# Absolute sums in the seven spatial groups: pieces of 512 elements become pieces of 1024, spread over more places

## The chip, the cores and the metric

The kernel runs on one core of a Trainium2 chip. The metric is device microseconds of one execution. The time before is 690.24 us, the median of 3 runs (690.11 to 691.26).

## What is computed

The reference mixes two branches over one input x of 2048 rows and 1024 columns: a dilated local attention (branch A) and a gated spatial MLP (branch B). The change lies in branch B and in how its last product is prepared.

```python
z = gelu(x @ w_in)                    # 2048 x 3584
z1, z2 = z[:, :1792], layernorm(z[:, 1792:])
g = w_sp @ z2 + b_sp[:, None]         # spatial product, 2048 x 2048 by 2048 x 1792
b = (z1 * g) @ w_out                  # 1792 x 1024
out = s * a + (1 - s) * b             # s = sigmoid(x . gate_w), a = attention
```

## The kernel before

The element product z1 * g is kept in SBUF as bfloat16, in tiles of 128 columns (14 of them, f = 0 to 13). For the first 1024 rows of the output it lies in two buffers, `z1c_slots[0]` and `z1c_slots[1]`, of 14 tiles x 512 rows each; the code calls this half v. For the other 1024 rows it lies in `u_late(f)`, 1024 rows a tile; the code calls this half u.

The last product with w_out uses a scheme of seven block products in place of eight (sums and differences of blocks), in 16-bit floats. To keep these sums in range, each half is first multiplied by a power of two. The power comes from the largest absolute row sum: ScalarE takes the sum of absolute values of each piece of u and v (an ACTIVATE with `ACT.Abs` and `accum_out`; each leaves a second, short instruction that reads the accumulator), VectorE takes the maximum of all pieces, and `whole_power` makes the power of two from it in three steps. The value itself need not be exact: it is a bound, and the scale is undone in `omg`.

Program order is fixed by hand (`tc.manual_schedule`): each engine runs its instructions in the order in which the code issues them, and waits for others by semaphores. Some work is handed out by `beat`, which keeps a planned time and issues an item when that time is reached; the absolute sums of the attention output (L412, 512 elements each) come in this way.

The change lies in the stage of `seven_products(n, extra)`, n = 0 to 6, the "spatial groups". A group computes tiles n and n + 7 of g for the last 1024 rows with seven products (L920) of eight matmuls each, all on TensorE:

1. product 1 into bank `pa`; ScalarE copies `pa` to `pb` (L943)
2. product 2 into `pe`; ScalarE copies it to `e5` (L945); then `extra(n, 1)`
3. product 3 adds to `pb`, so it waits for the copy L943; ScalarE copies `pb` to `pc` (L951), then fills two banks for the next group (L777)
4. product 4 adds to `pa`; ScalarE casts it to `gsb` (L956); then the u sums of the group before (L1012), and VectorE multiplies by z1 (`g_out`, L925); `extra(n, 2)`
5. product 5 adds to `pb`, so it waits until L951 has read it; VectorE adds `e5` (L963); `extra(n, 3)`
6. product 6 adds to `pc`; VectorE adds `e5` (L971); `extra(n, 4)`
7. product 7 adds to `pb`, so it waits until L963 has read it; ScalarE casts it (L980); `extra(n, 5)`

`extra(n, place)` puts other work between these steps: the scaling of w_out (L993) and its block sums on VectorE, loads, and the v sums (L1016). In groups 0 to 4, v sums stand at places 1 and 5, up to three in a row: place 1 for `z1c_slots[0]`, place 5 for `z1c_slots[1]`, tiles 3n to 3n + 2. Group 5 starts with the maximum of the v sums (L1229). The u sums of group n - 1 stand in group n behind L956, four in a row; those of group 6 come after the stage, beside `attn_pair(0)`, whose matmuls are L1127.

All absolute sums also write their absolute values to a scratch that nobody reads: `abs_out` (512 elements) or `abs_wide` (1024). `abs_wide` is used earlier by the row sums of the spatial weights (L848), which are ACTIVATEs of the same function over 1024 elements. Two further ACTIVATE-class lines of 1024 elements are L569 (absolute sums of a weight tile read with a stride) and L291 (a copy that permutes).

Of the kernel before, what the change touches and what calls it, by code (L numbers as in the profile page):

```python
# [10 lines left out]
F32 = mybir.dt.float32  # L11
# [4 lines left out]
P = 128  # L16
# [12 lines left out]
NF = FH // P  # L29
# [28 lines left out]
def kernel(  # L58
# [13 lines left out]
    nc = tc.nc  # L72
# [4 lines left out]
    sm = ctx.enter_context(tc.tile_pool(name="small", bufs=1))  # L77
# [5 lines left out]
    def reg(off, n):  # L83
        return arena[:, off:off + n]
# [13 lines left out]
    def warm_up(widths):  # L98
        pw = psum.tile([P, 512], F32, name="pw", tag="ps")
        for n in widths:  # L100
# [9 lines left out]
    s1 = sm.tile([P, 64], F32, name="s1")  # L110
# [12 lines left out]
    b_in = sm.tile([P, 8], BF, name="b_in")  # L123
    b_up = sm.tile([P, 8], BF, name="b_up")
    w_l1 = sm.tile([P, 7], F32, name="w_l1")
    v_l1 = s1[:, 0:28]
    u_l1 = sm.tile([P, 28], F32, name="u_l1")
    top = sm.tile([P, 1], F32, name="top")
    top_i = sm.tile([P, 1], I32, name="top_i")
    top_b = sm.tile([P, 1], BF, name="top_b")  # L130
# [57 lines left out]
    z1c_slots = [reg(CD_OFF + 8192, 7168).rearrange("p (f t) -> p f t", f=NF),  # L188
                 reg(EF_OFF + 8192, 7168).rearrange("p (f t) -> p f t", f=NF)]
# [3 lines left out]
    abs_out = reg(CD_OFF + 18944, 512)  # L193
    abs_wide = reg(EF_OFF + 15360, 1024)
# [261 lines left out]
    def load_wo(h):  # L456
        sync.dma_start(wo_sb[:, 4 * h:4 * h + 4, :], wo_d[4 * h:4 * h + 4].rearrange("g p n -> p g n"))

    def load_oT(a):
        sync.dma_start_transpose(oT_slots[a % 4], o_d[a * P:(a + 1) * P, :])  # L460
# [319 lines left out]
    def seed_group():  # L780
        seed(bsp_bc[:, 1024:1536])
        seed(bsp_more)
# [57 lines left out]
    def u_late(f):  # L840
        return u_first[:, f // 7] if f % 7 == 0 else z2[:, f - 1, 0:8, :]
# [49 lines left out]
    def t_sums(k):  # L891
        if k == 0:
            TT(t1, b_hi[:, 0:8], b_lo[:, 0:8], ALU.subtract)
        elif k == 1:
            TT(t3, b_hi[:, 8:16], b_hi[:, 0:8], ALU.subtract)
        elif k == 2:
            TT(t2, b_hi[:, 8:16], t1, ALU.subtract)
        else:
            TT(t4, b_lo[:, 8:16], t2, ALU.subtract)
        beat.on_vector(2.3)  # L900

    def s_sum(n, k):
        a11, a12 = z2[:, n, 0:8, :], z2[:, n, 8:16, :]
        a21, a22 = z2[:, n + 7, 0:8, :], z2[:, n + 7, 8:16, :]
        if k == 0:
            TT(sums[0], a21, a22, ALU.add)
        elif k == 1:
            TT(sums[1], sums[0], a11, ALU.subtract)
        elif k == 2:
            TT(sums[2], a11, a21, ALU.subtract)  # L910
        else:
            TT(sums[3], a12, sums[1], ALU.subtract)
        beat.on_vector(0.7)

    def bank():
        return psum.tile([P, 512], F32, name="ps", tag="ps")

    def product(dst, lhs, rhs):
        for k in range(8):
            nc.tensor.matmul(dst[:], lhs[:, k, :], rhs(k), start=False, stop=k == 7, skip_group_check=True)  # L920
        beat.run(8 * 512)

    def g_out(f, c, gsb):
        dst = u_late(f)[:, 4 * (c - 2):4 * (c - 1), :]
        TT(dst, gsb.rearrange("p (a q) -> p a q", a=4), dst, ALU.mult)  # L925
        beat.on_vector(0.43)

    def next_gsb():
        gs[0] += 1
        return gsb_slots[gs[0] % 3]  # L930

    def seven_products(n, extra):
        fa, fb = n, n + 7
        for f in (fa, fb):
            sync.dma_start(u_late(f).rearrange("p (c a) q -> p c (a q)", c=2),
                           z1_d[2:4, :, f * 512:(f + 1) * 512].rearrange("c p t -> p c t"))
        more = n + 1 < 7
        e5 = e5_slots[n % 2]
        extra(n, 0)
        pa, pe = seeded.pop(0), seeded.pop(0)  # L940
        product(pa, z2[:, fa, 0:8, :], lambda k: b_lo[:, k])
        pb = bank()
        nc.scalar.copy(pb[:], pa[:])  # L943
        product(pe, sums[0], lambda k: t1[:, k])
        nc.scalar.copy(e5, pe[:])  # L945
        if more:
            s_sum(n + 1, 0)
        extra(n, 1)
        product(pb, sums[1], lambda k: t2[:, k])
        pc = bank()  # L950
        nc.scalar.copy(pc[:], pb[:])  # L951
        if more:
            seed_group()
        product(pa, z2[:, fa, 8:16, :], lambda k: b_lo[:, 8 + k])
        gsb = next_gsb()
        nc.scalar.copy(gsb, pa[:])  # L956
        if n:
            u_sums(n - 1)
        g_out(fa, 2, gsb)
        extra(n, 2)  # L960
        product(pb, sums[2], lambda k: t3[:, k])
        gsb = next_gsb()
        TT(gsb, pb[:], e5, ALU.add)  # L963
        beat.on_vector(0.7)
        g_out(fb, 3, gsb)
        extra(n, 3)
        product(pc, sums[3], lambda k: b_hi[:, 8 + k])
        if more:
            s_sum(n + 1, 2)
        gsb = next_gsb()  # L970
        TT(gsb, pc[:], e5, ALU.add)  # L971
        beat.on_vector(0.7)
        g_out(fa, 3, gsb)
        extra(n, 4)
        product(pb, z2[:, fb, 8:16, :], lambda k: t4[:, k])
        if more:
            s_sum(n + 1, 1)
            s_sum(n + 1, 3)
        gsb = next_gsb()
        nc.scalar.copy(gsb, pb[:])  # L980
        g_out(fb, 2, gsb)
        extra(n, 5)
# [8 lines left out]
    def w_scale(f):  # L991
        for ff in (f, f + 7):
            nc.vector.tensor_scalar(w_out_sb[:, ff, :], w_out_sb[:, ff, :], w_up[:].bitcast(F32), None, ALU.mult)  # L993
        beat.on_vector(0.9)

    def w_sum(f, k):
        b11, b12, b21, b22 = w_tiles(f)
        if k == 0:
            TT(w_t(f, 0), b12, b11, ALU.subtract)
        elif k == 1:  # L1000
            TT(w_t(f, 1), b22, w_t(f, 0), ALU.subtract)
        elif k == 2:
            TT(w_t(f, 2), b22, b12, ALU.subtract)
        else:
            TT(w_t(f, 3), b21, w_t(f, 1), ALU.subtract)
        beat.on_vector(0.43)

    def u_sums(n):
        for h, f in enumerate((n, n + 7)):
            for k in range(2):  # L1010
                c = 4 * n + 2 * h + k
                nc.scalar.activation(abs_out.rearrange("p (i q) -> p i q", i=4), u_late(f)[:, 4 * k:4 * k + 4, :], ACT.Abs,  # L1012
                                     accum_out=u_l1[:, c:c + 1])

    def v_sum(c, f):
        nc.scalar.activation(abs_out, z1c_slots[c][:, f, :], ACT.Abs, accum_out=v_l1[:, 14 * c + f:14 * c + f + 1])  # L1016

    def u_rows(q, r, half):
        if q < 4:
# [62 lines left out]
    def wo_scale(h):  # L1082
        half = wo_sb[:, :, 512 * h:512 * h + 512]
        nc.vector.tensor_scalar(half, half, wo_up[:].bitcast(F32), None, ALU.mult)
# [127 lines left out]
    def extra(n, place):  # L1212
        if place == 1 and n == 0:
            t_sums(3)
        if place == 0 and n in (1, 3):
            part = slice(0, 11) if n == 1 else slice(11, NF)
            sync.dma_start(w_out_sb[:, part, :], wout_v[:, part, :])
        for k, f in enumerate(scale_sets.get(n, ())):
            if place == 2 + 2 * k:
                w_scale(f)  # L1220
        if place == 0:
            for f in sum_sets.get(n, ()):
                for k in range(4):
                    w_sum(f, k)
        if place in (1, 5) and n < 5:
            for f in range(3 * n, min(14, 3 * n + 3)):
                v_sum(place // 4, f)
        if n == 5 and place == 0:
            nc.vector.tensor_reduce(top[:], v_l1, AX.X, ALU.max)  # L1229
            next(v_steps)  # L1230
        if (n, place) in ((5, 3), (6, 0)):
            next(v_steps)
        if n == 2 and place == 5:
            nc.vector.tensor_reduce(top[:], o_l1[:], AX.X, ALU.max)
            next(o_steps)
        if (n, place) in ((3, 3), (4, 0)):
            next(o_steps)
        if n == 5 and place == 5:
            nc.scalar.copy(z2[:, 13, 0:8, :], u_first[:, 1])
        if n == 6 and place in (1, 2):  # L1240
            load_wo(place - 1)
        if n == 6 and place == 3:
            for r in range(4):
                load_oT(r)
            prepare(0)

    def prepare(q):
        u_scale(q)
        for k in range(4):
            u_sum(q, k)  # L1250
# [31 lines left out]
    for n in range(7):  # L1282
        seven_products(n, extra)
# [3 lines left out]
    prepare(1)  # L1287
    mix_pair(0)
    wo_scale(1)
    u_sums(6)  # L1290
    for k in range(4):
        wo_sum(k)
    attn_pair(0)
# [37 lines left out]
```

## Time and profile before

| | |
|---|---|
| median of 3 runs | 690.24 us (690.11 to 691.26) |
| profiled execution | 689.57 us, span in the trace 687.4 us |
| TensorE busy | 679.3 us, 99% of the span |
| VectorE busy | 564.6 us, 82% |
| ScalarE busy | 425.4 us, 62% |
| chain that ended last | PE 95%, ACT 3%, DMA 1% |
| spatial groups, products (L920) | 392 matmuls, from 459.1 to 549.1 us |
| v sums (L1016) | 28, from 463.2 to 526.0 us |
| u sums (L1012) | 28, from 481.1 to 564.1 us |

A row of the grouped view reads: line, engine, operation, output <- input with shapes, count | busy us, mean ns of one | idle time of the engine before them, and what ended most of it. A row of the timeline reads: start in us, duration in us, engine, line, operation, shapes, count, and in brackets the engine's idle time before it with what released it. A row of the waits reads: who <- for whom: us in total, times, longest us. A row of the windows reads: the stretch, its length, then busy time and count of each engine, the granted TensorE clock, and the DMA share.

### The profile page before, as it was taken

Reading aid. Unit: us, or ns where it says so; the run is one execution under the profiler, and the core shown is the slowest. Engines: PE = TensorE matmul, PEld = TensorE weight load, DVE = VectorE, ACT = ScalarE, POOL = GpSimd, SP = SyncE. Lnnn points to the kernel's source line nnn. Section 1 sums busy time; section 2 is a strip of 40 time slices with the busy share of each in tenths; the row PEclk is TensorE's granted clock in tenths of the full one; section 3 lists DMA queues with packets and bytes.
Section 4 is the critical chain, followed back from the end, with each engine's and each line's share of the span. In section 5 each row is a group of like instructions: output and inputs, shape, how many; then the busy total and the mean of one; then the engine's idle time right before and its main releaser. Section 6 shows DMA issues by size and latency. Waiting matters only on the chain.

```text
span 687.4 us, 9089 instructions
## 1 busy us (share of the span) xinstructions
PE 679.3 (99%) x3327; PEld 355.3 (52%) x3327; DVE 564.6 (82%) x701; ACT 425.4 (62%) x823; POOL 13.2 (2%) x45
## 2 busy tenths in 40 slices
PE   9999999999999999999999999999899999999997
PEld 4489666666654655444444444444344444444443
DVE  4649959999999997999998889994478888776653
ACT  4458767655566999759754997327987552223332
POOL 0000000000000022000000000000000000000000
PEclk9999999999999999999999999999999999999999
DMA  8995976554597308899978999918211413222210
GB/s 234 183 198 154 203 204 151 154 130 102 157 254 202 130 1 216 191 292 346 301 255 282 147 266 236 252 36 260 77 37 56 143 42 92 62 62 71 68 45 32
DMA packets 187996, 108.67 MB, mean 158 GB/s; under 512 B 146480, under 2 KB 172592, under 8 KB 187696
## 3 DMA queue, kind: packets, MB, share of 16 engines
q1 hardware_dynamic: 186224, 101.81, 57.1%
q10 hardware_dynamic: 1728, 6.29, 2.9%
q8 instruction: 26, 0.43, 0.2%
q14 instruction: 18, 0.15, 0.1%
HBM read 59.51 MB, written 34.41 MB: 137 GB/s over the span
## 4 chain that ended last, share of the span: by engine, by line
PE 95%; ACT 3%; DMA 1%; issue 0%; SPq 0%; DVE 0%; DVEq 0%; ACTq 0%
PE ps L617 16%; PE ps L302 14%; PE ps L829 14%; PE ps L802 14%; PE ps L1048 12%; PE ps L920 10%; PE ps L637 7%; PE ps L1137 6%; ACT arena L1016 1%; PE ps L1127 1%; ACT arena L412 1%; DMA arena<-in_B_w_in_dram 1%; ACT arena L1012 0%; PE po L506 0%; ACT ps L777 0%
## 5 line engine op out<-in xcount | busy, mean ns | idle before, releaser
L617 PE MATMUL ps<-arena 128*128 128x512 bf16 (+1 forms) x640 | 115.8, 337 | 0.0
L302 PE MATMUL ps<-arena 128*128 128x512 bf16 (+1 forms) x512 | 97.7, 353 | 0.2
L829 PE MATMUL ps<-arena 128*128 128x512 bf16 x448 | 97.7, 379 | 0.0
L617 PEld LDWEIGHTS <-arena 128*128 128x128 bf16 x640 | 83.1, 144 | 27.9 <-issue 0.5
L802 PE MATMUL ps<-arena 128*128 128x512 bf16 x448 | 97.0, 379 | 0.0
L1048 PE MATMUL ps<-arena 128*128 128x512 f16 (+1 forms) x392 | 92.8, 379 | 0.0
L920 PE MATMUL ps<-arena 128*128 128x512 bf16 (+1 forms) x392 | 85.9, 379 | 3.3 <-ACT ps L951 1.7
L302 PEld LDWEIGHTS <-arena 128*128 128x128 bf16 x512 | 50.1, 98 | 47.6 <-DVE arena L322 0.3
L348 DVE TENSOR_TENSOR arena<-arena 128x8192 bf16<-128x8192 bf16 x16 | 70.7, 4422 | 0.2
L802 PEld LDWEIGHTS <-arena 128*128 128x128 bf16 x448 | 43.7, 98 | 52.4
L391 DVE TENSOR_TENSOR arena<-arena,att_A 128x8192 bf16<-128x8192 bf16 x16 | 70.7, 4419 | 0.0
L829 PEld LDWEIGHTS <-arena 128*128 128x128 bf16 x448 | 43.5, 98 | 52.5 <-issue 0.5
L920 PEld LDWEIGHTS <-arena 128*128 128x128 bf16 (+1 forms) x392 | 38.0, 98 | 49.8 <-issue 4.4
L1048 PEld LDWEIGHTS <-arena 128*128 128x128 f16 (+1 forms) x392 | 38.3, 98 | 46.1
L623 ACT CAST arena<-ps 128x512 bf16<-128x512 f32 (+1 forms) x80 | 38.3, 508 | 32.1 <-PE ps L617 30.6
L351 DVE TENSOR_TENSOR arena<-arena 128x4096 bf16<-128x4096 bf16 (+1 forms) x32 | 56.2, 1755 | 0.8
L637 PE MATMUL ps<-arena 128*128 128x512 f16 (+1 forms) x224 | 52.4, 379 | 0.0
L307 ACT ACTIVATE arena<-ps 128x512 bf16<-128x512 f32 x64 | 34.2, 537 | 27.8 <-PE ps L302 27.8
L1137 PE MATMUL ps<-arena 128*128 128x512 f16 (+3 forms) x200 | 50.3, 375 | 0.0
L1117 DVE SCALAR_TENSOR_TENSOR arena<-ps,g_s,arena 128x512 bf16<-128x512 f32 (+2 forms) x33 | 24.0, 734 | 28.7 <-ACT arena L1169 19.9
L805 ACT ACTIVATE arena<-ps 128x512 bf16<-128x512 f32 x56 | 32.3, 599 | 20.4 <-PE ps L802 19.3
L637 PEld LDWEIGHTS <-arena 128*128 128x128 f16 (+1 forms) x224 | 32.2, 144 | 16.1
(204 smaller groups left out, 789.0 us busy)
## 6 DMA issues: line engine op xcount, KB each, us to landing
arena<-k_d SPq DMA_DIRECT2D x8, 960.0 KB, 7.0
arena<-v_d SPq DMA_DIRECT2D x8, 960.0 KB, 6.6
arena<-in_A_wqkv_dram SPq DMA_DIRECT2D x24, 256.0 KB, 4.9
z_d<-arena SPq DMA_DIRECT2D x12, 512.0 KB, 7.2
arena<-q_d SPq DMA_DIRECT2D x8, 512.0 KB, 3.8
o_d<-arena SPq DMA_DIRECT2D x4, 1024.0 KB
arena<-in_B_w_in_dram SPq DMA_DIRECT2D x4, 1024.0 KB
arena<-in_B_w_sp_dram ACTq DMA_DIRECT2D x8, 512.0 KB, 6.5
```

The costliest lines, as they stand in the source:

```text
L302: nc.tensor.matmul(ps[:, 0:N], xT[:, kt, i * P:(i + 1) * P], w2[c][:, kt, 0:N], start=(kt == 0), stop=(kt == KT - 1))
L348: TT(prod.rearrange("p (w j c) -> p w j c", w=W, j=8, c=C), in0, in1, ALU.mult)
L351: return lambda: TT(pv[:, :, 0:half], pv[:, :, 0:half], pv[:, :, half:2 * half], ALU.add)
L391: TT(prod.rearrange("p (w j d h) -> p w j d h", w=W, j=8, d=DH, h=HG), in0, in1, ALU.mult)
L617: nc.tensor.matmul(ps[:, n0:n1].rearrange("p (t c) -> p t c", c=C), lhsT, wgt[:, pos0:pos1, kt, :], start=(kt == 0), stop=(kt == KT - 1))
L623: nc.scalar.copy(slot[:, j % 4, n0:n1], ps[:, n0:n1])
L637: nc.tensor.matmul(dst[:].rearrange("p (t c) -> p t c", c=C), lhs(k), rhs[:, :, k, :], start=first and k == 0, stop=k == 3, skip_group_che ...
L802: nc.tensor.matmul(ps[:], w1[:, kt, (f % 4) * P:(f % 4 + 1) * P], xT[:, kt, 512 * c:512 * (c + 1)], start=(kt == 0), stop=(kt == KT - 1))
L829: nc.tensor.matmul(ps[:], z2[:, f, i, :], wsp[:, i, :, :].rearrange("p a t -> p (a t)"), start=False, stop=(i == 15), skip_group_check=True)
L920: nc.tensor.matmul(dst[:], lhs[:, k, :], rhs(k), start=False, stop=k == 7, skip_group_check=True)
L1048: nc.tensor.matmul(dst[:], lhs[:, j, :], rhs(j), start=first and j == 0, stop=j == 6, skip_group_check=not first)
L1137: nc.tensor.matmul(dst, lhs[:, k, :], rhs[:, k, :], start=first and k == 0, stop=k == 3, skip_group_check=not first)
```

## The change

Each absolute sum now covers 1024 elements and writes to `abs_wide`. A u sum covers one whole tile; a v sum covers two neighbouring tiles of a `z1c` buffer. So 28 + 28 ACTIVATEs become 14 + 14, and the two arrays of results have 14 columns instead of 28. The u sums of group n - 1 are parted: tile n - 1 stands behind L956 as before, tile n + 6 stands behind `extra(n, 4)`, ahead of product 7. The v sums stand one at a place, at places 1, 3 and 5: sums 3n to 3n + 2, of which 0 to 6 are in the first buffer and 7 to 13 in the second. The eight sums of the attention output (L412) in groups 1 and 2 stay between the same copies.

```diff
-    v_l1 = s1[:, 0:28]
-    u_l1 = sm.tile([P, 28], F32, name="u_l1")
+    v_l1 = s1[:, 0:NF]
+    u_l1 = sm.tile([P, NF], F32, name="u_l1")
...
         nc.scalar.copy(gsb, pa[:])
         if n:
-            u_sums(n - 1)
+            u_sums(n - 1, 0)
         g_out(fa, 2, gsb)
...
         extra(n, 4)
+        if n:
+            u_sums(n - 1, 1)
         product(pb, z2[:, fb, 8:16, :], lambda k: t4[:, k])
...
-    def u_sums(n):
-        for h, f in enumerate((n, n + 7)):
-            for k in range(2):
-                c = 4 * n + 2 * h + k
-                nc.scalar.activation(abs_out.rearrange("p (i q) -> p i q", i=4), u_late(f)[:, 4 * k:4 * k + 4, :], ACT.Abs,
-                                     accum_out=u_l1[:, c:c + 1])
-
-    def v_sum(c, f):
-        nc.scalar.activation(abs_out, z1c_slots[c][:, f, :], ACT.Abs, accum_out=v_l1[:, 14 * c + f:14 * c + f + 1])
+    def u_sums(n, h):
+        nc.scalar.activation(abs_wide.rearrange("p (i q) -> p i q", i=8), u_late(n + 7 * h), ACT.Abs,
+                             accum_out=u_l1[:, n + 7 * h:n + 7 * h + 1])
+
+    def v_sum(k):
+        nc.scalar.activation(abs_wide.rearrange("p (f t) -> p f t", f=2), z1c_slots[k // 7][:, 2 * (k % 7):2 * (k % 7) + 2, :],
+                             ACT.Abs, accum_out=v_l1[:, k:k + 1])
...
-        if place in (1, 5) and n < 5:
-            for f in range(3 * n, min(14, 3 * n + 3)):
-                v_sum(place // 4, f)
+        if place in (1, 3, 5) and n < 5 and 3 * n + place // 2 < NF:
+            v_sum(3 * n + place // 2)
...
-    u_sums(6)
+    u_sums(6, 0)
+    u_sums(6, 1)
```

## Prediction

> **What bounds the kernel now.** I read the page's busy shares first, then the windows of the stage that the change touches, then the waits of that stage.
>
> ```profile
> PE 679.3 (99%) x3327; PEld 355.3 (52%) x3327; DVE 564.6 (82%) x701; ACT 425.4 (62%) x823; POOL 13.2 (2%) x45
> ...
> L920 PE MATMUL ps<-arena 128*128 128x512 bf16 (+1 forms) x392 | 85.9, 379 | 3.3 <-ACT ps L951 1.7
> ...
> core 0: us, PE busy (x) PEld busy (x) DVE busy (x) ACT busy (x) POOL busy (x), PEclk, DMA share, GB/s
> 459.00:471.40 12.40, 12.40 (x60) 5.55 (x58) 9.93 (x13) 5.86 (x14) 0.00 (x0) 1.00 0.68 207
> 471.40:484.50 13.10, 12.23 (x57) 5.47 (x56) 4.90 (x11) 12.81 (x34) 0.00 (x0) 1.00 0.59 186
> 484.50:497.50 13.00, 10.53 (x49) 4.65 (x48) 4.26 (x9) 12.72 (x35) 0.00 (x0) 1.00 0.32 101
> 497.50:509.60 12.10, 12.10 (x58) 5.35 (x57) 8.26 (x22) 10.63 (x29) 0.00 (x0) 1.00 0.14 45
> ...
> PE ps L920 <- ACT ps L951: 1.7, 2, 0.9
> PE ps L920 <- ACT ps L943: 1.6, 1, 1.6
> ```
>
> TensorE is busy for 679.3 us of a 687.4 us span, so an edit on another engine pays only where TensorE waits for that engine. In the seven spatial groups (L920) it waits 3.3 us, all of it for two copies on ScalarE, and the windows say where: groups 1 and 2 (counted from 0), where ScalarE is busy for 12.8 of 13.1 and 12.7 of 13.0 us. In group 0 and from group 3 on TensorE does not wait. The granted clock is 1.00 in all of them, so it enters no sum.
>
> The idle time understates what the waits cost. A matmul is recorded with 379 ns, though the next one starts much sooner; the starts tell the true delay:
>
> ```profile
> 459.09 19.16 PE L920 MATMUL ps<-arena 128*128 128x512 bf16 x88
> 479.12 8.79 PE L920 MATMUL ps<-arena 128*128 128x512 f16 x40 [0.86 <-ACT ps L951]
> 489.51 3.61 PE L920 MATMUL ps<-arena 128*128 128x512 f16 x16 [1.60 <-ACT ps L943]
> 494.00 13.97 PE L920 MATMUL ps<-arena 128*128 128x512 f16 x64 [0.87 <-ACT ps L951]
> 507.90 0.22 PE L503 MATMUL po<-ident,top_b 128*1 128x128 bf16 x1
> ```
>
> Eighty-eight matmuls from 459.09 with the last one's 0.379 taken off give (19.16 - 0.379)/87 = 0.2158 us from start to start. A product of 8 lasts 1.726 us, a group of 56 12.09. Matmul 89 was due at 459.09 + 88 x 0.2158 = 478.08 and came at 479.12: 1.04 us late. In the same way 479.12 + 40 x 0.2157 = 487.75 against 489.51 (1.76 late), and 489.51 + 16 x 0.2158 = 492.96 against 494.00 (1.04 late). **The three waits cost 3.84 us**, not 3.3, and that is all that this change can win here. 88 = 56 + 32 says that the first is product 5 of group 1, which waits for the copy L951 of what product 3 left; the others are product 3 of group 2 (copy L943) and product 5 of group 2 (copy L951).
>
> **What ScalarE does in that time.** Its queue runs in order, and the copies stand behind absolute sums (L1016, L1012, and L412, which the change leaves alone).
>
> ```profile
> L1016 ACT ACTIVATE arena<-arena 128x512 bf16<-128x512 bf16 x28 | 17.6, 630 | 0.6
> L1012 ACT ACTIVATE arena<-arena 128x512 bf16<-128x512 bf16 x28 | 17.6, 630 | 0.7
> ...
> 461.02 0.57 ACT L943 COPY ps<-ps 128x512 f32<-128x512 f32 x1 [1.14 <-PE ps L920]
> 462.75 0.59 ACT L945 COPY arena<-ps 128x512 f32<-128x512 f32 x1 [1.16 <-PE ps L920]
> 463.23 0.63 ACT L1016 ACTIVATE arena<-arena 128x512 bf16<-128x512 bf16 x1
> ...
> 463.99 0.63 ACT L1016 ACTIVATE arena<-arena 128x512 bf16<-128x512 bf16 x1
> ...
> 464.74 0.63 ACT L1016 ACTIVATE arena<-arena 128x512 bf16<-128x512 bf16 x1
> ...
> 465.37 0.58 ACT L951 COPY ps<-ps 128x512 f32<-128x512 f32 x1
> ...
> 471.38 0.59 ACT L980 CAST arena<-ps 128x512 bf16<-128x512 f32 x1 [3.89 <-PE ps L920]
> ...
> 474.00 0.58 ACT L943 COPY ps<-ps 128x512 f32<-128x512 f32 x1
> ...
> 478.49 0.58 ACT L951 COPY ps<-ps 128x512 f32<-128x512 f32 x1
> ...
> 488.88 0.58 ACT L943 COPY ps<-ps 128x512 f32<-128x512 f32 x1
> ...
> 493.37 0.58 ACT L951 COPY ps<-ps 128x512 f32<-128x512 f32 x1
> ```
>
> A narrow sum holds the queue for 0.755 us when another sum follows (463.23 to 463.99 to 464.74) and 0.63 when a copy follows (464.74 to 465.37). A copy starts 1.93 us after its product does (461.02 - 459.09), which is the product's 1.73 and 0.20 more; TensorE goes on 0.05 after it (488.88 + 0.58 = 489.46, then 489.51).
>
> **The change part by part.** Each of the 28 + 28 narrow sums becomes half of a wide one; 28 wide ones remain. The trace has the wide one elsewhere: L848, same function, 1024 elements, with an accumulator, into the very scratch the change uses.
>
> ```profile
> 378.58 1.06 ACT L848 ACTIVATE arena<-arena 128x1024 bf16<-128x1024 bf16 x1
> ...
> 379.76 1.06 ACT L848 ACTIVATE arena<-arena 128x1024 bf16<-128x1024 bf16 x1
> ...
> 380.82 0.58 ACT L777 CAST ps<-arena 128x512 f32<-128x512 bf16 x1
> ...
> L848 ACT ACTIVATE arena<-arena 128x1024 bf16<-128x1024 bf16 x16 | 16.9, 1055 | 0.3
> L291 ACT COPY arena<-arena 128x1024 bf16<-128x1024 bf16 x8 | 15.7, 1997 | 0.0
> ...
> L569 ACT ACTIVATE arena<-arena 128x1024 bf16<-128x1024 bf16 x8 | 8.8, 1097 | 0.0
> ```
>
> It holds the queue for 1.18 us ahead of another sum and 1.06 ahead of a copy. Against 2 x 0.755 or 0.755 + 0.63 a pair saves 0.33 us; 28 pairs give 9.2 us of ScalarE, most of it where nobody waits. Bounds for one wide sum: 1.055 (L848) below, 1.097 (L569, strided input) near, and 1.997 (L291, same size, permuting) far above. I take L848's, since function, form and scratch are its own.
>
> The Trainium skill ("ScalarE: Activation LUTs", section "What ACT_TABLE_LOAD costs") gives an ACTIVATE with immediates 186 ns + 0.833 ns per element, overlapping its neighbour by 93 ns. By it alone a pair would save only the 93 ns, and it says nothing of the accumulator. L848's rows, at 0.33 us a pair, speak against it; what it would give is a rival below.
>
> Now the queue, in the changed kernel's order.
> - Group 1 begins at 459.09 + 12.09 = 471.18. L980 starts at 471.38 as before, one wide sum (three narrow before) follows it at 471.86 and frees ScalarE at 472.92. Copy L943 is then bound by its product: 471.18 + 1.93 = **473.11** (474.00 before).
> - L412 takes ScalarE to 474.24; L945 waits for product 2 until 471.18 + 3.45 + 0.20 = 474.83, a new idle time of 0.59. Wide sum at 475.30, L412 at 476.48, copy L951 at 477.11. It ends, with the 0.05, at 477.74; product 5 is due at 478.08. **The first wait goes**, 0.34 to spare.
> - From copy L943 of group 1 to that of group 2 ScalarE was never idle: 488.88 - 474.00 = 14.88 us. In between lie ten narrow sums of the two kinds (3 + 4 + 3) and six L412. Five wide ones save 1.65, the idle time gives back 0.59: 13.82 us, so the copy starts at 473.11 + 13.82 = 486.93 and TensorE goes on at 487.56. Product 3 of group 2 is due at 471.18 + 12.09 + 3.45 = 486.72. **The second wait shrinks from 1.76 to 0.84.**
> - Copy L943 to L951 in group 2 was 493.37 - 488.88 = 4.49; three narrow sums (2.27) become one wide (1.18): 3.40. L951 starts at 490.33, TensorE could go on at 490.96, and product 5 is due at 487.56 + 3.45 = 491.01. **The third wait goes**, but with 0.05 to spare.
> - Groups 0 and 3 to 6: behind L956 stand at most three wide sums (3.4 us) where four narrow ones (2.9) stood. Group 3 gives the cover: L956 starts as soon as product 4 has ended, 0.2 after product 5 begins, and L980 is due three products later, 5.2 us: 0.5 + 3.4 fit. The wide sum at place 5 ends 0.20 + 0.48 + 1.06 = 1.74 us into the next group, and the copy L943 behind it is ready at 1.93. Cost nothing; without cover a copy could still be 1.5 late before product 3 noticed.
> - What moves elsewhere: the orders of TensorE, GpSimd and SyncE's queue are unchanged, no DMA moves. On VectorE two maxima read 14 columns for 28, and a wait of the fourth Wo sum (L1098) for the old scratch goes. The last u sums run beside L1127's matmuls. All nothing.
>
> Next late is VectorE's L963, which reads what product 7 then adds to:
>
> ```profile
> 494.92 0.57 ACT L956 CAST arena<-ps 128x512 bf16<-128x512 f32 x1
> ...
> 495.52 0.43 DVE L925 TENSOR_TENSOR arena<-arena 128x512 bf16<-128x512 bf16 x1 [6.88 <-ACT arena L956]
> 495.87 0.88 DVE L993 TENSOR_SCALAR arena<-arena,w_up 128x1024 bf16<-128x1024 bf16 x2
> 496.66 0.68 DVE L963 TENSOR_TENSOR arena<-ps,arena 128x512 bf16<-128x512 f32 x1
> ```
>
> Product 7 of group 2 was due at 494.00 + 3.45 = 497.45 and L963 ended at 497.34. L956 came 0.92 after product 5; now it comes at 490.33 + 1.55 = 491.88, 0.87 after it. The cover of 0.11 holds, barely.
>
> **Sum.** 3.84 - 0.84 = 3.0 us, all on TensorE's chain, which runs from there to the end without another wait for ScalarE. The profiled execution took 689.57 us, 2.17 more than its span of 687.4; it becomes 686.6, with a span of 684.4. The median of the runs shown, 690.24, lies 0.67 above that execution and becomes **687.2**, which I give.
>
> **The rivals.**
> - *All three waits go* (gain 3.84, 686.4 on the median). It needs the six L412 in that stretch to be placed 0.84 us lighter, and their order is fixed. Chance 0.04.
> - *Pairs save little.* At 0.093 a pair instead of 0.33 the stretch saves 0.47 and not 1.65, so the second wait is about 2.0 and the third 0.2: gain 1.6, 688.6. It is the rate of the ScalarE page; L848 speaks against it. Chance 0.08.
> - *VectorE takes over.* L963 stands behind L956, L925 and two L993 with 0.11 to spare; if L963 comes 0.5 later against product 5 than I reckon, it passes its cover by 0.4, and groups 2 to 6 give back five times that, 2.0 us: gain 1.0, 689.2, not to be told from no change. Against it: L956 comes no later than before relative to product 5. Or the change does not shorten the queue at all. Chance 0.09.
> - *Slower: a wide sum as dear as L291.* At 1.997 each is 0.94 longer. The stretch to copy L943 of group 2 gains five of these, less the 0.59 of idle time that they fill: its wait becomes about 5.0; the two copies L951 wait 0.8 and 0.9, copy L943 of group 3 some 2.1. That is 8.8 for 3.84, **5 us slower, 695.2**. It decides from about 1.5 us a wide sum on. For it: a row of this size on this engine does take 2 us, and behind the cast L956 three such would stand in a row. Against it: those permute, L848 does not. Chance 0.05.
>
> **How the numbers follow.** Forecast 0.74, rivals 0.04, 0.08, 0.09, 0.05. Inside the forecast the near bound of 1.097 adds 5 x 0.04 = 0.2 to the wait. A measurement of this kernel tells about 0.2%, 1.4 us, from no change; the first three cases lie beyond it: faster 0.86, same 0.09, slower 0.05. The range goes from 686.0 (all waits gone, counted half from the profiled execution's 689.57, half from the median) to 689.3 (the VectorE rival), leaving out the slower case and the tails.
>
> **What the changed kernel's profile would show.** Wide sums near 1.055 us; no wait of TensorE for L951; one wait for L943, about 0.7 of idle time in the record (0.84 late by the starts), at product 3 of group 2; ScalarE's narrow share in groups 1 and 2 still near full. Wrong would be a wait of TensorE for VectorE at product 7, a wait in group 3 or later, or sums well over 1.1 us.

## The result and the profile after

The median went from 690.11 us (689.97 to 691.26, 6 runs) to **686.28 us** (685.84 to 686.97, 6 runs), 3.83 us less: a ratio of 0.9943 with a 95% interval of 0.9931 to 0.9956. The profiled execution took 685.84 us with a span of 683.7, against 689.57 and 687.4 before.

From the page of the changed kernel: busy time by engine, the chain that ended last, and the row of the spatial products.

```profile
PE 676.1 (99%) x3276; PEld 355.4 (52%) x3327; DVE 564.2 (83%) x701; ACT 417.1 (61%) x767; POOL 13.2 (2%) x45
...
PE 97%; DMA 1%; issue 0%; SPq 0%; ACT 0%; DVE 0%; DVEq 0%
...
L920 PE MATMUL ps<-arena 128*128 128x512 f16 (+1 forms) x385 | 84.9, 379 | 0.6 <-issue 0.3
```

ScalarE's part in the chain that ended last has gone from 3% to nothing, and no idle time for ScalarE is left in the L920 row. (7 of the 392 matmul records are missing from this trace, so its counts and small idle times are rough; the starts are not.) ScalarE lost 8.3 us of busy time, of which TensorE's chain got 3.7.

The timeline of TensorE in the changed kernel; columns are start, duration, line, shapes, count.

```profile
459.06 45.21 PE L920 MATMUL ps<-arena 128*128 128x512 bf16 x205
504.20 0.22 PE L503 MATMUL po<-ident,top_b 128*1 128x128 bf16 x1
...
545.18 10.74 PE L1048 MATMUL ps<-arena 128*128 128x512 bf16 x48
```

Three breaks have become one unbroken run. From the first L920 to the first L1048 the stage takes 545.18 - 459.06 = **86.12 us**. In the kernel before, the products began at 459.09, and its timeline has L1048 at 548.87:

```profile
548.87 10.74 PE L1048 MATMUL ps<-arena 128*128 128x512 bf16 x49
```

That is 89.78 us: 3.66 us of the 3.7 that the span lost are here. This length is the yardstick below, since it leaves out what scatters elsewhere.

ScalarE's timeline of the changed kernel: the copies that TensorE waits for, and some of the sums between them (L1015 is v, L1011 is u, both wide; L412 is narrow).

```profile
473.08 0.57 ACT L943 COPY ps<-ps 128x512 f32<-128x512 f32 x1
...
475.29 1.06 ACT L1015 ACTIVATE arena<-arena 128x1024 bf16<-128x1024 bf16 x1
476.25 0.19 ACT L1015 ACTIVATION_READ_ACCUMULATOR arena<-arena 128x1 f32 x1
476.34 0.62 ACT L412 ACTIVATE arena<-arena 128x512 bf16<-128x512 bf16 x1
...
476.95 0.59 ACT L951 COPY ps<-ps 128x512 f32<-128x512 f32 x1
...
480.64 0.62 ACT L412 ACTIVATE arena<-arena 128x512 bf16<-128x512 bf16 x1
...
481.25 1.05 ACT L1015 ACTIVATE arena<-arena 128x1024 bf16<-128x1024 bf16 x1
482.20 0.19 ACT L1015 ACTIVATION_READ_ACCUMULATOR arena<-arena 128x1 f32 x1
482.42 1.06 ACT L1011 ACTIVATE arena<-arena 128x1024 bf16<-128x1024 bf16 x1
...
486.22 0.58 ACT L943 COPY ps<-ps 128x512 f32<-128x512 f32 x1
...
489.48 0.58 ACT L951 COPY ps<-ps 128x512 f32<-128x512 f32 x1
```

The first copies came nearly as forecast (L943 at 473.08, forecast 473.11; L951 at 476.95, forecast 477.11). Copy L943 of group 2 came at 486.22, 0.71 us earlier than forecast. With its 0.58 and 0.05 it frees TensorE at 486.85, and product 3 of group 2 was due at 459.06 + 128 x 0.2158 = 486.68: a delay of 0.17 us, where I had 0.84. It is too short to leave a gap between the recorded matmuls; e5 below shows it in the length of the run.

The rows show why. Ahead of another wide sum a wide one holds the queue for 482.42 - 481.25 = 1.17 us, as forecast. Ahead of L412 it holds it for 476.34 - 475.29 = 1.05, not 1.18, and L412 ahead of a wide sum for 481.25 - 480.64 = 0.61, not 0.755. In the changed kernel L412 still writes `abs_out` while the wide sums write `abs_wide`. So the suspicion after the result was: the 0.13 us that I had taken as the price of one sum behind another is the price of writing the *same scratch* as the sum before.

### The profile page after: what moved, and what is told of

Its sections match the earlier page's. It is cut to its first block, busy times and chain, and to the rows that moved or that the text cites. A ratio compares the mean times of both kernels' runs of the same rounds, so it can differ in the third digit from the quotient of the medians.

```text
span 683.7 us, 8977 instructions
## 1 busy us (share of the span) xinstructions
PE 676.1 (99%) x3276; PEld 355.4 (52%) x3327; DVE 564.2 (83%) x701; ACT 417.1 (61%) x767; POOL 13.2 (2%) x45
## 4 chain that ended last, share of the span: by engine, by line
PE 97%; DMA 1%; issue 0%; SPq 0%; ACT 0%; DVE 0%; DVEq 0%
PE ps L617 16%; PE ps L829 14%; PE ps L802 14%; PE ps L302 14%; PE ps L920 12%; PE ps L1048 12%; PE ps L637 7%; PE ps L1137 6%; PE ps L1127 1%; DMA arena<-in_B_w_in_dram 1%; PE po L506 0%; SPq L523 0%; PE po L503 0%; SPq L521 0%; SPq L519 0%
## 5 line engine op out<-in xcount | busy, mean ns | idle before, releaser
L617 PE MATMUL ps<-arena 128*128 128x512 bf16 (+1 forms) x637 | 115.6, 337 | 0.2
L302 PE MATMUL ps<-arena 128*128 128x512 bf16 (+1 forms) x501 | 97.3, 352 | 0.7
L1048 PE MATMUL ps<-arena 128*128 128x512 f16 (+1 forms) x380 | 91.2, 379 | 0.5
L920 PE MATMUL ps<-arena 128*128 128x512 f16 (+1 forms) x385 | 84.9, 379 | 0.6 <-issue 0.3
L1048 PEld LDWEIGHTS <-arena 128*128 128x128 f16 (+1 forms) x392 | 38.3, 98 | 46.1
L920 PEld LDWEIGHTS <-arena 128*128 128x128 bf16 (+1 forms) x392 | 38.0, 98 | 46.1 <-issue 0.5
L637 PE MATMUL ps<-arena 128*128 128x512 f16 (+1 forms) x224 | 52.4, 379 | 0.0
```

The lines of the kernel that those rows point to most:

```text
L302: nc.tensor.matmul(ps[:, 0:N], xT[:, kt, i * P:(i + 1) * P], w2[c][:, kt, 0:N], start=(kt == 0), stop=(kt == KT - 1))
L617: nc.tensor.matmul(ps[:, n0:n1].rearrange("p (t c) -> p t c", c=C), lhsT, wgt[:, pos0:pos1, kt, :], start=(kt == 0), stop=(kt == KT - 1))
L637: nc.tensor.matmul(dst[:].rearrange("p (t c) -> p t c", c=C), lhs(k), rhs[:, :, k, :], start=first and k == 0, stop=k == 3, skip_group_che ...
L1048: nc.tensor.matmul(dst[:], lhs[:, j, :], rhs(j), start=first and j == 0, stop=j == 6, skip_group_check=not first)
```

## The experiments

The kernels below differ in three things: the width of the u and v sums, their places, and the scratch. The two theories at the start: **queue length** (TensorE's delay is what stands in ScalarE's queue ahead of L943 and L951, and the scratch adds 0.13 to a step), against **accumulator or width** (the 0.13 hangs on the array of results or on the width) and against the places alone doing the work. The stage lengths are in the table. "L412 apart" means that the u and v sums write one scratch and L412 another. Each ratio is to executions of the kernel before that were taken along with that run (medians 690.07 us for e1 to e4, 690.00 for e5 to e7).

| kernel | sums | places | scratch | stage, us | median, us | ratio to before, 95% interval |
|---|---|---|---|---|---|---|
| before | narrow | old | one | 89.78 | 690.11 | |
| e3 | narrow | new | one | 88.74 | 689.92 | 0.9989, 0.9972 to 1.0007 |
| e2 | narrow | old | two in turn | 87.51 | 687.66 | 0.9959, 0.9942 to 0.9976 |
| e7 | narrow | new | two in turn | 86.90 | 687.49 | 0.9955, 0.9940 to 0.9970 |
| e4 | wide | old | L412 apart | 86.87 | 687.13 | 0.9961, 0.9937 to 0.9985 |
| e1 | wide | new | one | 86.83 | 687.06 | 0.9950, 0.9933 to 0.9966 |
| after | wide | new | L412 apart | 86.12 | 686.28 | 0.9943, 0.9931 to 0.9956 |
| e5 | wide | new | two in turn | 85.97 | 685.85 | 0.9931, 0.9906 to 0.9955 |
| e6 | wide, each twice | new | L412 apart | 101.50 | 701.32 | 1.0149, 1.0115 to 1.0184 |

### e1: the changed kernel with one scratch

```diff
-                abs_out.rearrange("p (j c) -> p j c", j=2), obuf[:, 2 * k:2 * k + 2, :], ACT.Abs,
+                (abs_wide[:, 0:512] if g + 1 == NG else abs_out).rearrange("p (j c) -> p j c", j=2), obuf[:, 2 * k:2 * k + 2, :], ACT.Abs,
```

> The changed kernel, but the last eight sums over the attention output (L412, those in groups 1 and 2) write to the same scratch as the wide sums. Theory (scratch): a sum that writes the scratch of the sum just before it starts about 0.12 us later than one that writes another. Then a wide sum holds the queue for about 1.18 us ahead of L412 (1.05 in the changed kernel), product 3 of group 2 comes 0.87 us late instead of 0.16, and the time is 0.7 us above the changed kernel's, about 687.0. Rival (accumulator): the extra 0.12 comes from another accumulator array, or from the width; then the steps stay at 1.05 and the time at 686.3.

ScalarE's timeline of e1, a wide sum and the L412 behind it, then TensorE's timeline:

```profile
476.24 1.06 ACT L1015 ACTIVATE arena<-arena 128x1024 bf16<-128x1024 bf16 x1
...
477.42 0.63 ACT L412 ACTIVATE arena<-arena 128x512 bf16<-128x512 bf16 x1
```

```profile
460.02 27.79 PE L920 MATMUL ps<-arena 128*128 128x512 bf16 x128
488.51 17.43 PE L920 MATMUL ps<-arena 128*128 128x512 f16 x80 [0.71 <-ACT ps L943]
...
546.85 9.44 PE L1048 MATMUL ps<-arena 128*128 128x512 bf16 x43
```

The step is back at 477.42 - 476.24 = 1.18 us, though L412 still adds up into its own array: it is the scratch, and neither the accumulator nor the width. Product 3 of group 2 was due at 460.02 + 128 x 0.2158 = 487.64 and came at 488.51, 0.87 late, exactly the theory's figure (and the prediction's 0.84). The stage took 0.71 us more than in the changed kernel, the median 0.78.

### e2: the kernel before with two scratches

```diff
+    def scratch():
+        turn[0] += 1
+        return abs_out if turn[0] % 2 else abs_wide[:, 0:512]
...
-        nc.scalar.activation(abs_out, z1c_slots[c][:, f, :], ACT.Abs, accum_out=v_l1[:, 14 * c + f:14 * c + f + 1])
+        nc.scalar.activation(scratch(), z1c_slots[c][:, f, :], ACT.Abs, accum_out=v_l1[:, 14 * c + f:14 * c + f + 1])
```

The u sums and the last eight sums of the attention output take `scratch()` in the same way.

> The kernel before, its 56 narrow sums where they were, but these and the last eight L412 write in turn to two scratches of 512. Theory (scratch): a narrow sum ahead of another holds the queue for 0.63 us instead of 0.755; the three delays of TensorE (1.04, 1.76, 1.04) become about 0.4, 0.7 and 0.6, 1.7 in all, and the time falls by 2.1 us to about 688.0. Rival (accumulator or width): the step stays 0.755 and the time 690.1.

In e2's timelines all lines after the helper are 6 higher (L1022 is the v sum, L926 the product, L949 and L957 the copies). First ScalarE, then TensorE:

```profile
475.54 0.63 ACT L1022 ACTIVATE arena<-arena 128x512 bf16<-128x512 bf16 x1
...
476.16 0.62 ACT L1022 ACTIVATE arena<-arena 128x512 bf16<-128x512 bf16 x1
```

```profile
459.31 19.16 PE L926 MATMUL ps<-arena 128*128 128x512 bf16 x88
478.62 8.79 PE L926 MATMUL ps<-arena 128*128 128x512 f16 x40 [0.15 <-ACT ps L957]
487.88 3.61 PE L926 MATMUL ps<-arena 128*128 128x512 f16 x16 [0.46 <-ACT ps L949]
491.94 13.97 PE L926 MATMUL ps<-arena 128*128 128x512 f16 x64 [0.45 <-ACT ps L957]
```

The narrow step falls from 0.755 to 0.62 us, and the three delays, worked out as before, to 0.32, 0.63 and 0.61, 1.56 in all (1.7 expected). So 2.3 us of the kernel's 3.84 could be had with no change of width or place.

### e3: the new places, with narrow sums

```diff
-        if place in (1, 5) and n < 5:
-            for f in range(3 * n, min(14, 3 * n + 3)):
-                v_sum(place // 4, f)
+        if place in (1, 3, 5) and n < 5 and 3 * n + place // 2 < NF:
+            k = 3 * n + place // 2
+            for f in (2 * (k % 7), 2 * (k % 7) + 1):
+                v_sum(k // 7, f)
```

The u sums are parted between the two places as in the changed kernel.

> The changed kernel's places with narrow sums in one scratch: two of 512 where one of 1024 stands. Theory (all of it is the length of ScalarE's queue ahead of the copies): the first delay goes, since only two narrow sums and no more than one L412 stand ahead of each copy L943 and L951 of group 1; product 3 of group 2 is 2.4 us late, product 5 of group 2 about 0.3; 2.7 in all against 3.84, time about 689.0. Rival (the places alone do it): no delay, 686.3. Rival (places do nothing): 690.1.

TensorE's timeline of e3 (L1050 is the L1048 of the changed kernel):

```profile
459.67 27.79 PE L920 MATMUL ps<-arena 128*128 128x512 bf16 x128
489.80 17.70 PE L920 MATMUL ps<-arena 128*128 128x512 f16 x80 [2.34 <-ACT ps L943]
...
548.41 7.93 PE L1050 MATMUL ps<-arena 128*128 128x512 bf16 x36
```

Product 3 of group 2 is 489.80 - 487.29 = 2.51 us late. The 80 matmuls behind it last 17.70 us where e1's last 17.43, which is the second delay of 0.28 at product 5 (copy L951 began at 492.90). Together 2.79, against 2.7 expected: moving the sums takes the first wait away (1.04), makes the second 0.75 longer and the third 0.76 shorter.

The time is less clear: the median of twelve executions is 689.92, and by the medians alone e3 cannot be told from the kernel before. The executions fall into two groups of six. Those from 688.62 to 689.57 list a mean granted clock of 0.999 or 1.000, those from 690.26 to 690.80 one of 0.997 or 0.998. My estimate from these figures: a mean that is 0.002 to 0.003 lower is what some 3 to 4 us at a clock of 0.50 would give, and that would cost 1.4 to 2.1 us; the means of the two groups lie 1.65 us apart. So in half of its executions e3 seems to lose to the clock what it wins by the places. The profiled execution (689.06, against 689.0 expected) is of the first group and no trace of the second was kept, so that the wait of 2.34 us brings the lower clock on is not shown. The verdict on the places rests on the stage of the profiled execution.

### e4: wide sums at the old places

```diff
-        if place in (1, 3, 5) and n < 5 and 3 * n + place // 2 < NF:
-            v_sum(3 * n + place // 2)
+        if place in (1, 5) and n < 5:
+            for k in ((3 * n,), (3 * n + 1, 3 * n + 2))[place // 4]:
+                if k < NF:
+                    v_sum(k)
```

Both u sums stand behind L956.

> The changed kernel's wide sums, but at the places of before: both u sums behind the cast L956, and the v sums at places 1 and 5 only (one at place 1, two at place 5). Theory (queue length): product 3 of group 2 comes about 0.8 us late, and product 3 of groups 1, 3 and 4 about 0.1 each, since two wide sums stand ahead of copy L943 there; 1.05 in all, time about 687.2. Rival (the width alone does it): 686.3. Rival (the places matter as much as the width): over 688.

TensorE's timeline of e4 (L1047 is the L1048 of the changed kernel):

```profile
459.49 27.88 PE L920 MATMUL ps<-arena 128*128 128x512 bf16 x128
487.94 17.52 PE L920 MATMUL ps<-arena 128*128 128x512 f16 x80 [0.56 <-ACT ps L943]
...
546.36 9.88 PE L1047 MATMUL ps<-arena 128*128 128x512 bf16 x45
```

By the start, product 3 of group 2 is 0.83 late (487.94 against 487.11), with some 0.1 of it lost already in group 1: there copy L943 began at 474.50, two wide sums behind its cast, and held product 3 until 475.13, 0.10 after its due time. The stage is 0.75 us longer than in the changed kernel (0.9 expected). The new places are thus worth 0.75 us once the sums are wide, and 1.04 when they are narrow.

### e7: the new places, narrow sums, two scratches

e3, with e2's `scratch()` for all narrow sums:

```diff
-                nc.scalar.activation(abs_out.rearrange("p (i q) -> p i q", i=4), u_late(f)[:, 4 * k:4 * k + 4, :], ACT.Abs,
+                nc.scalar.activation(scratch().rearrange("p (i q) -> p i q", i=4), u_late(f)[:, 4 * k:4 * k + 4, :], ACT.Abs,
```

> The changed kernel's places with narrow sums, these and the last eight L412 writing in turn to two scratches of 512. Theory (queue length): with steps of 0.62 us two narrow sums hold the queue for 1.24 us against 1.05 to 1.18 of a wide one; product 3 of group 2 about 1.0 us late, nothing else; the stage takes about 87.0 us (88.7 with one scratch), time about 687.1. Rival (the scratch counts only ahead of old places): no less than 2 us late, time 688.5 or more.

TensorE's timeline of e7, and from ScalarE's the copy that releases it (its lines are 6 to 8 higher: L949 is L943, L1056 the L1048 of the changed kernel):

```profile
460.46 27.79 PE L926 MATMUL ps<-arena 128*128 128x512 bf16 x126
489.03 17.43 PE L926 MATMUL ps<-arena 128*128 128x512 f16 x79 [0.77 <-DVE arena L912]
...
547.36 10.74 PE L1056 MATMUL ps<-arena 128*128 128x512 bf16 x48
```

```profile
488.40 0.58 ACT L949 COPY ps<-ps 128x512 f32<-128x512 f32 x1
```

The row names VectorE, whose L912 ended at the same 488.98 as the copy. But the instruction that waited carries in the kept trace a wait on the semaphore that ScalarE raises and on no other, as in e3, and the copy's end and the 0.05 give 489.03 to the digit: it is the same wait, with the wrong name. The first product began at 460.46, so product 3 was due at 488.08 and is 0.95 late (1.0 expected); the stage is 86.90 (87.0 expected).

### e5: wide sums in two scratches

```diff
+    abs_wide_2 = reg(CD_OFF + 18432, 1024)
...
+        return abs_wide_2 if turn[0] % 2 else abs_wide
```

All wide sums and the last eight L412 take them in turn.

> The changed kernel, with all its wide sums and the last eight L412 writing in turn to two scratches of 1024. Theory (scratch): wide sums step 1.05 us also ahead of another wide sum; the two such steps ahead of copy L943 of group 2 give it 0.12 to 0.25 us, so the last delay of TensorE (product 3 of group 2, 0.16 us in the changed kernel) goes to about nothing. The stage from the first spatial product to the first product of the last stage is 86.0 us against 86.1: no difference that the times can show, 686.2. Rival (TensorE is still held by ScalarE elsewhere in the stage): more than 0.2 us less.

ScalarE's timeline of e5 (L1022 is v, L1018 u): the step between wide sums.

```profile
481.54 1.05 ACT L1022 ACTIVATE arena<-arena 128x1024 bf16<-128x1024 bf16 x1
482.49 0.19 ACT L1022 ACTIVATION_READ_ACCUMULATOR arena<-arena 128x1 f32 x1
482.58 1.05 ACT L1018 ACTIVATE arena<-arena 128x1024 bf16<-128x1024 bf16 x1
```

1.04 us where it was 1.17. TensorE's timeline (L927 is the product, L1055 the L1048 of the changed kernel):

```profile
459.36 45.07 PE L927 MATMUL ps<-arena 128*128 128x512 bf16 x205
...
545.33 10.74 PE L1055 MATMUL ps<-arena 128*128 128x512 bf16 x48
```

The stage takes 85.97 us, 0.15 less than the changed kernel's. The unbroken run of 208 matmuls (3 records missing in both traces) lasts 45.07 us where the changed kernel's lasted 45.21, and 207 x 0.2158 + 0.379 = 45.05 is what it takes with no delay: the last delay is gone, and no ScalarE wait is left to remove there. In the times (685.85 against 686.28, with overlapping intervals) it cannot be told from the changed kernel.

### e6: each wide sum twice

```diff
+        for _ in range(2):
+            nc.scalar.activation(abs_wide.rearrange("p (i q) -> p i q", i=8), u_late(n + 7 * h), ACT.Abs,
+                                 accum_out=u_l1[:, n + 7 * h:n + 7 * h + 1])
```

The v sums likewise.

> The changed kernel with every wide sum of u and v taken twice in a row, into the same result: the second repeats the first and is superfluous. A sum then holds the queue for about 2.2 us. Theory (queue length, the slower rival of the prediction with its price): product 5 of group 0 about 0.1 late, copies L951 of groups 1 and 2 make product 5 about 1.0 late each, product 3 is about 5.4 late in group 2 and about 3 late in groups 3 and 4; some 13 us in all, the stage takes about 99.5 us and the time is near 699.5. Rival (slack that the arithmetic does not know, or a limit elsewhere): under 6 or over 18 us.

TensorE's timeline of e6, then windows of it (stretch, its length, busy time of PE, PEld, DVE, ACT and POOL, granted clock, DMA share, GB/s):

```profile
459.19 19.34 PE L920 MATMUL ps<-arena 128*128 128x512 bf16 x87
479.36 8.79 PE L920 MATMUL ps<-arena 128*128 128x512 f16 x39 [0.83 <-ACT ps L951]
493.34 14.98 PE L920 MATMUL ps<-arena 128*128 128x512 f16 x55 [5.19 <-ACT ps L943]
510.50 5.34 PE L920 MATMUL ps<-arena 128*128 128x512 f16 x24 [2.17 <-DVE arena L1007]
...
525.41 19.23 PE L920 MATMUL ps<-arena 128*128 128x512 f16 x79 [1.99 <-DVE arena L1003]
...
560.69 10.74 PE L1050 MATMUL ps<-arena 128*128 128x512 bf16 x48
```

```profile
493.30:498.40 5.10, 5.06 (x12) 1.73 (x12) 0.00 (x0) 5.07 (x12) 0.00 (x0) 0.50 0.04 17
498.40:499.20 0.80, 0.80 (x4) 0.38 (x3) 0.00 (x0) 0.37 (x1) 0.00 (x0) 0.69 0.00 0
499.20:500.20 1.00, 1.00 (x7) 0.42 (x5) 0.00 (x0) 0.47 (x1) 0.00 (x0) 1.00 0.00 0
```

At the first two waits the queue does what the arithmetic says: 0.83 and 5.19 us of idle time (about 1.0 and 5.35 by the starts) for L951 of group 1 and L943 of group 2, where 1.0 and 5.4 were expected. The two waits whose rows name VectorE are for L943 again, in groups 3 and 4: the copies began at 509.87 and 524.78, with 0.63 more that is 510.50 and 525.41, and both waiting matmuls carry in the kept trace a wait on ScalarE's semaphore alone.

But the whole stage is 15.4 us longer than the changed kernel's, where 13.4 were expected, and the parts are other ones. After the wait of 5.19 us the granted clock is 0.50 for 5.1 us and 0.69 for 0.8 more. The 56 matmuls that begin there (one record is missing) last 14.98 us where 55 x 0.2158 + 0.379 = 12.25 would do, 2.73 more; the lost clock, 5.10 x 0.50 + 0.80 x 0.31 = 2.80, accounts for them. A second such stretch (last section) lengthens the last 80 from e1's 17.43 to 19.23, 1.80 more. So the clock, which the arithmetic left out, costs some 4.5 us. The waits for ScalarE add up to only 0.19 + 0.99 + 5.35 + 2.34 + 2.17 = 11.0: L943 of groups 3 and 4 cost 2.3 and 2.2 where about 3 each were expected, and the 1.0 expected at L951 of group 2 does not show. Both together are 15.6, against the 101.50 - 85.97 = 15.5 by which the stage is longer than e5's. A TensorE at half clock is also due later, which would make its waits shorter; that this is all of the difference was not tried.

## Why the prediction was right, and where its size was off

- **What bounds the stage: right.** Three waits, worth 3.84 us by the starts and not the 3.3 of the idle column. The stage with no delay left (e5) is 89.78 - 85.97 = 3.81 us shorter, so the reading by starts is shown.
- **The price of a wide sum: right.** 1.058 us (L1015) and 1.057 (L1011) on average, against 1.055 taken from L848. The bound from L291 (1.997) did not apply.
- **First wait gone, third wait gone: right.** TensorE's unbroken run shows it.
- **Second wait shrinks to 0.84: wrong in size.** It shrank to 0.17. The step that failed reads "Five wide ones save 1.65, the idle time gives back 0.59: 13.82 us". Measured from copy to copy it was 486.22 - 473.08 = 13.14. The five wide sums were priced, by L848 and by narrow sums in a row, as if every sum behind a sum paid 0.13 us. In all those rows both write one scratch. The change also moves the u and v sums to another scratch than L412's, which I had noted only for the wait of L1098. In that stretch a wide sum meets L412, ahead of it or behind it, five times; five times 0.13 is the missing 0.68 but for 0.03. e1, which takes back only this, brings the 0.87 back.
- **The rival "all three waits go"** was nearer to the result (686.4 against 686.28) than the forecast (687.2). I gave it 0.04 because L412's order is fixed; its order is, but not its price. The reason was wrong. That the time lies in the range is owed to this rival at its lower end: nothing reckoned in the forecast itself led to a smaller second wait. Of the 0.96 us between forecast and result, 0.67 are this wait, 0.13 the median before (690.24, then 690.11 with more runs), and the rest lies outside the stage.
- **Groups 0 and 3 to 6 cost nothing: right, but the cover was overstated.** "A copy could still be 1.5 late before product 3 noticed" leaves out the copy's own 0.58 and the 0.05: 3.45 - 1.93 - 0.63 = 0.89. e4 shows it: copy L943 of group 1 began 2.93 us into its group, 1.00 later than 1.93, and product 3 was 0.10 late.
- **Pairs save little:** refuted as a forecast. The Trainium skill ("ScalarE: Activation LUTs", section "What ACT_TABLE_LOAD costs") has 0.833 ns per element for an ACTIVATE, and the trace agrees: (1.04 - 0.62)/512 is 0.82 ns from e5's and e2's steps. The same section of the Trainium skill has neighbouring ACTIVATEs overlap by about 93 ns, and the changed kernel's rows agree from record to record: 476.25 is 0.10 us ahead of 475.29 + 1.06, and 476.34 is 0.10 ahead of 476.25 + 0.19. But the short instruction that reads the accumulator, 0.19 us, lies between two sums and uses up both overlaps, so that from sum to sum nothing of it is left. A pair saves 2 x 0.62 - 1.04 = 0.20 us with two scratches and 0.33 within one, not 0.093.
- **VectorE takes over: did not come.** In the changed kernel's VectorE timeline L963 of group 2 began at 492.78 and took 0.68; product 7 was due at 459.06 + 160 x 0.2158 + 0.17 = 493.76, so its cover grew from 0.11 to 0.30:

```profile
492.78 0.68 DVE L963 TENSOR_TENSOR arena<-ps,arena 128x512 bf16<-128x512 f32 x1
```

- **Slower, with dear sums:** the mechanism holds where the sums are really that dear. e6, with 2.2 us a sum, is 15.0 us above the changed kernel and 11.2 above the one before, some 4.5 of it by the clock. The rival's own price (2.0 us a sum, 5 us slower) was not tried.
- **What each part was worth** (stage, from 89.78): places alone 1.04, second scratch alone 2.27, wide sums at the old places with L412 apart 2.91, wide sums at the new places in one scratch 2.95, all as changed 3.66. The width by itself, at the new places, is worth 88.74 - 86.83 = 1.91 with one scratch and 86.90 - 85.97 = 0.93 with two in turn; at the old places with one scratch it was not tried. The parts do not add up: each shortens the same queue, and only delay ahead of L943 and L951 counts.

## What to carry to other kernels

Where an in-order helper engine holds the copies that TensorE waits for, write out its queue from copy to copy with the steps (start to start) and not the durations, and take TensorE's delay from its matmul starts. When a step is read off a row, note what its neighbour writes: a scratch that nobody reads still held back the next sum that wrote it, and two of them used in turn were worth 2.3 us here without another edit.

## What the runs showed of the hardware

- A sum that writes the scratch of the sum just before it starts 0.12 to 0.14 us later: narrow steps 0.755 against 0.62 (e2), wide steps 1.18 against 1.05 (e1 against the changed kernel), 1.17 against 1.04 (e5). With another scratch the next sum starts 0.10 us ahead of the end of the accumulator read (476.34 against 476.25 + 0.19); with the same one it starts 0.03 behind it (482.42 against 482.20 + 0.19). In the kept traces these sums carry a wait on the semaphore that ScalarE itself raises, which fits a wait of the compiled program for the engine's own earlier write to the same bytes. The value that they wait for is not kept, so this is inferred; whether the chip would need such a wait was not tried.
- TensorE's granted clock fell to 0.50 after a wait of 5.19 us, for about 5 us. In the profiled execution of e3 a wait of 2.34 us left it at 1.00 (six of e3's other executions list a lower mean, without a trace). In e6 a wait of 2.17 us left it at 1.00 too, but about 1 us after one of 1.99 it was at 0.50 for 3 us:

```profile
525.40:526.40 1.00, 0.99 (x5) 0.46 (x5) 0.93 (x5) 1.00 (x2) 0.00 (x0) 0.90 0.00 0
526.40:527.40 1.00, 1.00 (x4) 0.38 (x3) 0.90 (x6) 0.97 (x3) 0.00 (x0) 0.50 0.00 0
527.40:528.40 1.00, 1.00 (x3) 0.30 (x2) 0.38 (x1) 0.83 (x3) 0.00 (x0) 0.50 0.00 0
528.40:529.40 1.00, 1.00 (x4) 0.40 (x3) 0.00 (x0) 1.00 (x3) 0.00 (x0) 0.50 0.00 0
529.40:530.40 1.00, 1.00 (x6) 0.42 (x5) 0.00 (x0) 0.47 (x1) 0.00 (x0) 0.89 0.00 0
```

  The Trainium skill ("TensorE: Matmul & The Clock Gate", section "Part 1: The HAM clock gate (the "warmup" mystery)") has the clock at half after an idle window of about 3.4 us. The 5.19 us agree with it. The drop after 1.99 us does not follow from it, and its cause stays open.
